# One load of the first batch's queries and keys for both attentions, pooled scores and value products in tiles of the array, and a new order

## The chip, the cores and the metric

The kernel runs on one core of a Trainium2 chip. The metric is the device time of one execution in microseconds; less is better. The core's engines are TensorE (PE), VectorE (DVE), ScalarE (ACT), GpSimd (POOL) and SyncE (SP), which issues most transfers here. Each engine runs its instructions in the order of the program and waits for the others through semaphores.

## The reference

Inputs `q`, `k`, `v` have shape (4, 8, 576, 64): batch, heads, sequence, head size.

```python
def _attn_ref(q, k, v):
    factor = 4
    # pooled: means over 4 tokens, full softmax attention over 144 positions, each result used for 4 tokens
    q_d, k_d, v_d = (x.reshape(B, H, Sd, factor, D).mean(axis=3) for x in (q, k, v))
    out_up = np.repeat(sm_attn(q_d, k_d, v_d), factor, axis=2)
    # local: each token attends to the 7 tokens with |distance| < 4
    mask = np.abs(pos[:, None] - pos[None, :]) < factor
    out_local = softmax(where(mask, scale * q @ k.T, -1e9)) @ v
    return out_up + out_local

x = attn_out.transpose(0, 2, 1, 3).reshape(2304, 512)
x = np.maximum(x @ w_in1, 0) ** 2 @ w_out1      # 512 -> 2048 -> 512
out = softplus(x @ w_in2) @ w_out2              # 512 -> 2048 -> 512
```

## The kernel before

One program does the attention and two MLP layers. The MLP's numbers are split into a high and a low half, so each product is three matmuls.

- **Token groups.** The 2304 tokens fall into five groups of `BLOCKS = [8, 6, 8, 8, 6]` blocks of 64. `STEPS` lists the MLP's work: a layer, a group and one of 16 slices of the hidden layer. `hidden` does a step's 12 hidden matmuls (tile `ph`), `activate` the activation and its high and low halves (`gh`, `gl`), and `outputs` the 12 output matmuls (`y`).
- **Weights.** `load_weights` loads half slices as raw 64-bit numbers (`raw`, three buffers, 512 KB each); `weight_job` converts one in seven instructions of ScalarE and VectorE (`f`, `r`, `w`) into a slot, and stores it to `wdram`, from where `weight_again` loads it for later uses.
- **Pooled attention** (`pooled`). 16 tasks, one for each batch and pair of heads. It sums queries and keys over four tokens (on VectorE, or for batch 1 on TensorE as `pqk`), makes two masked copies of the query sums (`qd`, with the constant `diag`, so that each holds one head's 64 rows and zeros), takes three score matmuls of 96 by 144 (`psc`), the softmax (`pn`, `pe`), six transposes (`ppp`), and two matmuls with the summed values (`vd`, `ppo`). Both heads' rows come out of one product, so a copy for each head picks its half into `up`.
- **Local attention** (`local`). 14 tasks, one for each block of groups 0 and 1. For four pairs of heads: scores in 64x64 tiles of the array (`lsc`), mask and softmax (`ls`, `ln`, `le`), transposes (`lpp`, `lpt`), four value products (`lav`), of which again each head's half is used, added to `up` on 64 partitions at a time (`lt`), and split into `xh` and `xl`, the MLP's input. Queries, keys and values of two blocks are one load each (`lq`, `lk`, `lv`). The tokens of groups 2 to 4 have local attention without matmuls (`direct`).
- **First buffers.** `lend` lets first loads use slots of weights and of inputs that are not needed yet.
- **The order.** Nothing is scheduled on the chip. While the program is built, the class `Order` follows a model of the engines and transfers: each stream says which engine it wants and for how long (`t_act`, `t_dve`, constants), `landed` models a transfer, and the piece that can start first is issued next. `either` lets it choose ScalarE or VectorE for a copy. The lists `POOLED` and `LOCAL` say from which step on a task may start. The model sets the order alone; the durations on the chip are what they are.

Of the kernel before, what the change touches and what calls it, by code (L numbers as in the profile page):

```python
# [28 lines left out]
KH = SP // 2  # L29
NF = DFF // 128  # L30
# [38 lines left out]
LOCAL = [(-18.9, -13), (-0.5, 5), (12, 58), (62, 86), (74, 92)]  # L69
# [16 lines left out]
WIN, HOT, COLD = 3.413, 3.1, 1.8  # L86

# [78 lines left out]
class Order:  # L166
# [66 lines left out]

def t_act(n):
    return 0.09 + n * 0.84e-3
# [12 lines left out]
def fused_kernel(ctx: ExitStack, tc: tile.TileContext, lq, lk, lv, dqk, dv, cdmask, pqk, pv, wts, cmask, cdiag, cident, out):  # L248
# [15 lines left out]
    diag = const.tile([128, 2], F32, name="diag")  # L264
# [12 lines left out]
    r_in = ring(att, "in", [128, 2 * S], BUFS["in"])  # L277
# [3 lines left out]
    r_qd = ring(att, "qd", [128, 2 * SP], 2)  # L281
# [17 lines left out]
    def copy(out, in_, scale=1.0):  # L299
        if order.chosen == "act":  # L300
            act.activation(out=out, in_=in_, func=AF.Copy, scale=scale)  # L301
        elif isinstance(scale, float):
            dve.tensor_copy(out=out, in_=in_)  # L303
        else:
            dve.tensor_scalar(out=out, in0=in_, scalar1=scale, scalar2=None, op0=ALU.mult)
# [139 lines left out]
    def lend():  # L445

        for p in range(LENT):
# [3 lines left out]
            x, y = both[:, :1024], both[:, 1024:]  # L451
            if p < NP:
                first_bufs["q", p] = Guest(x[:, :2 * NP * QB], lent[k])
                first_bufs["v", p] = Guest(y[:KH], lent[k])
            else:
                first_bufs["pv", 0] = Guest(x[:KH], lent[k])
        for p, r in enumerate((r_xh[1], r_xl[1])):
# [3 lines left out]
            first_bufs["in", 2 + p] = Guest(x[:, :2 * S], host)  # L461
            first_bufs["k", p] = Guest(x[:, 2 * S:2 * S + 2 * NP * KW], host)
# [6 lines left out]

    loads_direct = Event()  # L470
# [17 lines left out]
    def load_tasks():  # L488
        todo = [(mask, cmask)]
        for x, y in ((diag, cdiag), (ident, cident)):  # L490
            t = yield "sp", 0.06
            sp.dma_start(out=x, in_=y)
            order.landed(t, 65536)
        for (kind, at, hp, i, _), ev in zip(tasks, arrived, strict=True):
            if kind == "d":
                continue
            if kind == "l":
# [17 lines left out]
            else:  # L515
                two = at * NP + hp
                t = yield "sp", 0.06, *room(r_in, "in", two)
                ev.buf = take_for(r_in, "in", two)
                sp.dma_start(out=ev.buf.tile, in_=pqk[at * NP + hp])
                ev.at = order.landed(t, 128 * 4 * 2 * S)  # L520
# [24 lines left out]
    def pooled(b, hp, banks, ev, pace):  # L545

        on_pe = b in SUMS_ON_PE
# [540 lines left out]
```

## Time and profile before

| | |
|---|---|
| Median of 3 runs | 913.7 us (911.52 to 915.76) |
| Profiled execution | 916.07 us, of which the span of the instructions is 914.3 us |
| Busy: TensorE, VectorE, ScalarE, GpSimd | 882.6, 628.9, 507.8, 70.0 us |
| Granted TensorE clock, mean | 0.991 of full speed |
| Data moved by DMA | 179.51 MB |

A busy share is an average over stages. The rows further down are from this execution; times in them are us from the start of its span, and what a row calls PEld is the load of a matmul's fixed operand.

### The profile page before, as it was taken

To read this page: it belongs to the slowest core of one execution; us is meant where nothing else is said; L and a number is where in the kernel's file an instruction comes from. 1 tells how busy PE (TensorE), PEld (TensorE's weight loads), DVE (VectorE), ACT (ScalarE), POOL (GpSimd) and SP (SyncE) were. 2 spreads that over 40 slices of the span, in tenths; PEclk is the share of its full clock that TensorE was granted. 3 is DMA by queue.
4 is the path that set the end of the run, shared out by engine and by line. 5 is a ranking of instruction groups with operands and counts; after the bars stand their busy time and mean duration, and the time that the engine had idled before them with its cause. 6 is when DMAs were issued, how large, how long until landed. Compare 5 with 4: busy or idle time off the path is not lost.

```text
span 914.3 us, 12634 instructions
## 1 busy us (share of the span) xinstructions
PE 882.6 (97%) x4528; PEld 764.1 (84%) x4528; DVE 628.9 (69%) x1105; ACT 507.8 (56%) x1141; POOL 70.0 (8%) x136
## 2 busy tenths in 40 slices
PE   2989999999999999999999999999999999999997
PEld 2778879998888878888888888888999888988886
DVE  3798997899999999998777998986211224222222
ACT  3877876766887886554344544443333325544443
POOL 0000000000000000121111121101120010000000
PEclk9799999999999999999999999999999999999999
DMA  8958968884956873597776577740870262233001
GB/s 215 261 184 270 317 213 310 272 296 149 351 192 220 273 275 151 183 335 261 237 256 224 171 250 242 261 153 30 297 249 24 74 202 94 63 99 127 24 0 47
DMA packets 50091, 179.51 MB, mean 196 GB/s; under 512 B 5762, under 2 KB 6146, under 8 KB 50028
## 3 DMA queue, kind: packets, MB, share of 16 engines
q1 hardware_dynamic: 31020, 109.48, 35.6%
q0 software_dynamic: 19008, 69.21, 23.4%
q8 instruction: 36, 0.59, 0.3%
q14 instruction: 27, 0.22, 0.1%
HBM read 140.40 MB, written 38.27 MB: 195 GB/s over the span
## 4 chain that ended last, share of the span: by engine, by line
PE 83%; DVE 7%; DMA 6%; ACT 3%; issue 1%; SPq 0%; ACTq 0%
PE ph L861 39%; PE y L915 39%; DMA raw<-wts 3%; DMA first<-lk 1%; DMA w_first<-lq 1%; PE ppo L622 1%; DVE lt L701 1%; PE psc L580 1%; DVE f L375 1%; ACT le L669 1%; DVE vd L617 1%; ACT f L366 1%; PE ppp L608 1%; DVE xl L316 1%; PE dpp L803 1%
## 5 line engine op out<-in xcount | busy, mean ns | idle before, releaser
L861 PE MATMUL ph<-xh,w 128*128 128x512 f32 (+2 forms) x1304 | 397.4, 367 | 2.9 <-ACT xh L301 1.4
L861 PEld LDWEIGHTS ph<-xh,w 128*128 128x128 f32 x1304 | 240.9, 188 | 35.5 <-ACT xh L301 2.0
L861 PE MATMUL ph<-xl,w 128*128 128x512 f32 (+2 forms) x652 | 237.8, 365 | 1.0 <-DVE xl L316 1.0
L915 PE MATMUL y<-gh,w 128*128 128x512 f32 (+2 forms) x656 | 200.0, 367 | 0.0
L915 PE MATMUL y<-w,gh 128*128 128x512 f32 x576 | 179.5, 393 | 0.0
L316 DVE TENSOR_TENSOR gl<-g,gh 128x512 fp32r<-128x512 f32 (+2 forms) x163 | 101.9, 625 | 91.4 <-ACT gh L301 87.9
L861 PEld LDWEIGHTS ph<-xl,w 128*128 128x128 f32 x652 | 122.6, 188 | 16.9 <-DVE xl L316 1.4
L915 PEld LDWEIGHTS y<-gh,w 128*128 128x128 f32 x656 | 121.0, 188 | 14.4
L410 POOL DMA_DIRECT2D w<-wdram x132 | 69.8, 532 | 777.2 <-PE dpp L803 377.9
L915 PEld LDWEIGHTS y<-w,gh 128*128 128x128 f32 x576 | 106.7, 188 | 20.5
L915 PE MATMUL y<-gl,w 128*128 128x512 f32 (+2 forms) x328 | 119.1, 363 | 0.0
L915 PE MATMUL y<-w,gl 128*128 128x512 f32 x288 | 112.6, 391 | 0.0
L301 ACT ACTIVATE gh<-g 128x512 fp32r<-128x512 f32 (+2 forms) x127 | 72.8, 573 | 70.5 <-PE y L915 50.3
L884 DVE SCALAR_TENSOR_TENSOR g<-ph,g 128x512 f32<-128x512 f32 (+2 forms) x81 | 50.7, 626 | 89.1 <-ACT g L882 89.0
L878 ACT ACTIVATE g<-ph 128x512 f32<-128x512 f32 (+2 forms) x81 | 44.4, 549 | 117.0 <-PE ph L861 108.1
L873 ACT ACTIVATE g<-ph 128x512 f32<-128x512 f32 (+2 forms) x82 | 44.4, 542 | 112.5 <-PE ph L861 92.3
L915 PEld LDWEIGHTS y<-gl,w 128*128 128x128 f32 x328 | 61.7, 188 | 6.8
L915 PEld LDWEIGHTS y<-w,gl 128*128 128x128 f32 x288 | 54.1, 188 | 11.6
L366 ACT ACTIVATE f<-raw 128x512 f32<-128x512 f32 x64 | 42.6, 667 | 23.4 <-DMA raw<-wts 18.3
L303 DVE CAST gh<-g 128x512 fp32r<-128x512 f32 (+2 forms) x36 | 14.8, 410 | 51.2 <-PE y L915 43.5
L753 DVE TENSOR_TENSOR prod<-dqk 128x896 f32<-128x896 f32 x44 | 47.6, 1083 | 1.6 <-DMA dqk<-dqk 1.3
L876 ACT ACTIVATE g<-g 128x512 f32<-128x512 f32 (+2 forms) x82 | 47.4, 578 | 1.9
(99 smaller groups left out, 961.2 us busy)
## 6 DMA issues: line engine op xcount, KB each, us to landing
w<-wdram POOLq DMA_DIRECT2D x132, 512.0 KB, 4.3
raw<-wts SPq DMA_DIRECT2D x64, 512.0 KB
wdram<-w SPq DMA_DIRECT2D x64, 512.0 KB
dqk<-dqk SPq DMA_DIRECT2D x11, 896.0 KB
in<-pqk SPq DMA_DIRECT2D x14, 576.0 KB
dv<-dv SPq DMA_DIRECT2D x11, 640.0 KB
out<-o SPq DMA_DIRECT2D x18, 256.0 KB
pv<-pv SPq DMA_DIRECT2D x15, 288.0 KB
```

The lines of the kernel that those rows point to most:

```text
L301: act.activation(out=out, in_=in_, func=AF.Copy, scale=scale)
L303: dve.tensor_copy(out=out, in_=in_)
L316: dve.tensor_tensor(out=out, in0=whole, in1=high.bitcast(F32), op=ALU.subtract)
L366: act.activation(out=f.tile, in_=high.bitcast(F32), func=AF.Abs, scale=REBIAS)
L410: nc.gpsimd.dma_start(out=weights[slot][:, half], in_=wdram[c, half])
L753: dve.tensor_tensor(out=p4, in0=k4[:, :, tok:tok + TAPS, :], in1=q4[:, tok].unsqueeze(2).to_broadcast([128, 2, TAPS, D]), op=ALU.mult)
L861: pe.matmul(ph.tile[:, :n], w, y, start=(k == 0), stop=(k == len(prs) - 1))
L873: act.activation(out=o, in_=h, func=AF.Relu)
L876: act.activation(out=o, in_=o, func=AF.Square)
L878: act.activation(out=o, in_=h, func=AF.Abs)
L884: dve.scalar_tensor_tensor(out=o, in0=h, scalar=0.0, in1=o, op0=ALU.max, op1=ALU.add)
L915: pe.matmul(o, wt, y, start=(begin and k == 0), stop=(end and k == 2))
```

## The change

- The first batch's queries and keys were loaded twice: once for the pooled tasks (`pqk`) and once in blocks for the eight local blocks of group 0 (`lq`, `lk`). Now `pqk` carries three zero columns between queries and keys (`QKW = S + FCT - 1`), and the eight blocks read their queries and windows of keys from the four pooled tiles. These four loads come first in SP's queue, and each local block of group 0 waits for all four. The tiles lie in lent weight slots, with the sums and the softmax of the same task beside them.
- The pooled scores are six matmuls, each of one head's 64 rows and 64 query columns, instead of three on masked copies; `qd` and `diag` are gone. The three windows of 64 queries overlap and start 40 apart; 48 columns of each are used.
- The pooled and the local value products run per head, on 64 columns of the array, so both heads' results land on their own partitions: one copy into `up` and one addition into `lt` instead of two each.
- The planner's numbers change: slower transfers, 32 columns more for an MLP matmul, shorter pieces of TensorE, and the first entry of `LOCAL`.

```diff
-LOCAL = [(-18.9, -13), (-0.5, 5), (12, 58), (62, 86), (74, 92)]
+LOCAL = [(-17, -13), (-0.5, 5), (12, 58), (62, 86), (74, 92)]
...
-        self.dma = max(self.dma, self.issue + 0.65) + size / 3.6e5
-        return self.dma + 0.9
+        self.dma = max(self.dma, self.issue + 1.2) + size / (2.4e5 if self.dma < CROWDED else 3.3e5)
+        return self.dma + 1.3
...
+def t_pe(n):
+    return (n + 32) / 2.4e3
...
-                first_bufs["q", p] = Guest(x[:, :2 * NP * QB], lent[k])
-                first_bufs["v", p] = Guest(y[:KH], lent[k])
+                first_bufs["in", p] = Guest(both[:, :2 * QKW], lent[k])
+                first_bufs["in", p].left = 1 + BLOCKS[0]
+                s0 = 2 * QKW
+                first_bufs["qkd", p] = Guest(both[:, s0:s0 + 2 * SP], lent[k])
+                first_bufs["pe", p] = Guest(both[:, s0 + 2 * SP:s0 + 5 * SP], lent[k])
             else:
-                first_bufs["pv", 0] = Guest(x[:KH], lent[k])
+                for two in range(2):
+                    first_bufs["v", two] = Guest(both[:KH, two * 1024:two * 1024 + 1024], lent[k])
         for p, r in enumerate((r_xh[1], r_xl[1])):
             b = r.take("first")
             host = Host(b)
             x = b.tile.bitcast(F32).rearrange("p h n -> p (h n)")
-            first_bufs["in", 2 + p] = Guest(x[:, :2 * S], host)
-            first_bufs["k", p] = Guest(x[:, 2 * S:2 * S + 2 * NP * KW], host)
+            for two in range(2):
+                first_bufs["pv", 2 * p + two] = Guest(x[:KH, two * 1024:two * 1024 + 1024], host)
...
+        for p, ev in enumerate(first_pairs):
             t = yield "sp", 0.06
-            sp.dma_start(out=x, in_=y)
-            order.landed(t, 65536)
+            ev.buf = first_bufs["in", p]
+            sp.dma_start(out=ev.buf.tile, in_=pqk[p])
+            ev.at = order.landed(t, 128 * 8 * QKW)
...
+            if kind == "l" and not i:
+                if at % 2 == 0:
+                    t = yield "sp", 0.06, *room(r_v, "v", at // 2)
+                    bv = take_for(r_v, "v", at // 2)
+                    bv.left = 2
+                    sp.dma_start(out=bv.tile[:KW], in_=lv[at // 2])
+                    vthere = order.landed(t, KW * 4096)
+                ev.buf = None, None, bv, at % 2
+                ev.at = 0.0
+                ev.v.at = vthere
...
-            copy(qk3[:, 1], src[:, 1])
+            t = yield either, t_either(288)
+            copy(qk.tile, sums.tile[:, :2 * SP])
...
-        qd4 = qd.tile.rearrange("p (i a q) -> p i a q", i=3, a=2)
-        for a in range(2):
-            t = yield either, (0.31, 0.28)
-            copy(qd4[:, :, a, :], src[:, 0, :].rearrange("p (i q) -> p i q", i=3), scale=diag[:, a:a + 1])
-        if on_pe:
-            sums.free = t
-        t = yield "pe", 0.75, banks
+            t = yield "dve", t_dve(1152), ev, pace, *room(r_s, "qkd", two), *room(r_e, "pe", two), r_n
+            qk, e, n = take_for(r_s, "qkd", two), take_for(r_e, "pe", two), r_n.take("pn")
+            x4 = halves().rearrange("p a (g j) -> p a g j", j=FCT)
+            dve.tensor_reduce(out=qk.tile.rearrange("p (a g) -> p a g", a=2), in_=x4, axis=AX.X, op=ALU.add)
+            if b:
+                ev.buf.free = t
+            else:
+                used_once(t, ev.buf)
+
+        t = yield "pe", 0.5, banks
         sc = bank(banks, "psc")
-        sc3 = sc.tile[:96, :3 * SP].rearrange("p (i k) -> p i k", i=3)
+        sc3 = sc.tile[:, :3 * SP].rearrange("p (i k) -> p i k", i=3)
         for i in range(3):
-            pe.matmul(sc3[:, i, :], qd4[:, i].rearrange("p a q -> p (a q)"), qk3[:, 1, :], start=True, stop=True)
-        qk.free = qd.free = t
+            for p in (slice(0, 64), slice(64, 128)):
+                pe.matmul(sc3[p, i, :], qk.tile[p, i * RUN:i * RUN + 64], qk.tile[p, SP:], start=True, stop=True)
+        qk.free = t
...
-                pe.transpose(pp.tile[:KH, i * 96:(i + 1) * 96], e3[:96, i, a * KH:(a + 1) * KH], ident[:96, :96])
+                pe.transpose(pp.tile[:KH, i * 128:(i + 1) * 128], e3[:, i, a * KH:(a + 1) * KH], ident)
...
-            copy(pt3[:, a, :], pp.tile[:KH, :288])
+            used = pp.tile[:KH, :3 * (176 - RUN)].rearrange("p (i x) -> p i x", i=3)
+            used = used[:, :, :128].rearrange("p i (h q) -> p i h q", h=2)[:, :, :, :48]
+            copy(pt3[:, a, :].rearrange("p (i h q) -> p i h q", i=3, h=2), used)
...
-        t = yield "pe", 0.98, banks
+        t = yield "pe", 0.66, banks
         po = bank(banks, "ppo")
         for a in range(2):
-            pe.matmul(po.tile[:, :288], vd.tile[:, a, :], pt3[:, a, :], start=(a == 0), stop=(a == 1))
+            pt4 = pt3[:, a, :].rearrange("p (i h q) -> p h i q", i=3, h=2)
+            for h in range(2):
+                pe.matmul(po.tile[64 * h:64 * h + 64, :SP], vd.tile[:, a, 64 * h:64 * h + 64], pt4[:, h],
+                          start=(a == 0), stop=(a == 1))
         vd.free = pt.free = t
-        for j in range(2):
-            t = yield either, t_either(144)
-            p0 = 64 * j
-            copy(ups[b].tile[p0:p0 + 64, hp, :].rearrange("p (i q) -> p i q", i=3),
-                 po.tile[p0:p0 + 64, :288].rearrange("p (i a q) -> p i a q", i=3, a=2)[:, :, j, :])
+        t = yield either, t_either(144)
+        copy(ups[b].tile[:, hp, :], po.tile[:, :SP])
...
-        t = yield "pe", 0.86, ev, pace, banks, r_s, r_e, r_n, r_t
+        t = yield "pe", 0.62, ev, pace, banks, r_s, r_e, r_n, r_t, *([] if i else first_pairs)
         sc, s, e, n, o = bank(banks, "lsc"), r_s.take("ls"), r_e.take("le"), r_n.take("ln"), r_t.take("lt")
         bq, bk, bv, at = ev.buf
-        q = bq.tile.rearrange("p (w q) -> p w q", q=QB)
+        if i:
+            qs = [bq.tile[:, w * QB:w * QB + QB] for w in range(at * NP, at * NP + NP)]
+            ks = [bk.tile[:, w * KW:w * KW + KW] for w in range(at * NP, at * NP + NP)]
+        else:
+            qs = [x.buf.tile[:, blk * QB:blk * QB + QB] for x in first_pairs]
+            ks = [x.buf.tile[:, S + blk * QB:S + blk * QB + KW] for x in first_pairs]
         sc4 = sc.tile[:, :NP * KW].rearrange("p (h k) -> p h k", h=NP)
         for h in range(NP):
-            w = at * NP + h
             for p in (slice(0, 64), slice(64, 128)):
-                pe.matmul(sc4[p, h], q[p, w], bk.tile[p, w * KW:w * KW + KW], start=True, stop=True)
-        used_once(t, bq, bk)
+                pe.matmul(sc4[p, h], qs[h][p], ks[h][p], start=True, stop=True)
+        used_once(t, *((bq, bk) if i else (x.buf for x in first_pairs)))
...
-            pe.matmul(av.tile[:, h * 128:(h + 1) * 128], bv.tile[:KW, (at * NP + h) * 128:(at * NP + h + 1) * 128],
-                      pt.tile[:KW, h * 128:(h + 1) * 128], start=True, stop=True)
+            for a in range(2):
+                v0, q0 = (at * NP + h) * 128 + a * 64, h * 128 + a * QB
+                pe.matmul(av.tile[a * 64:a * 64 + 64, h * QB:(h + 1) * QB], bv.tile[:KW, v0:v0 + 64],
+                          pt.tile[:KW, q0:q0 + QB], start=True, stop=True)
...
-        for hh in range(2):
-            t = yield "dve", t_dve(256), up_ready[b]
-            p = slice(64 * hh, 64 * hh + 64)
-            dve.tensor_tensor(out=o4[p], in0=av5[p, :, hh], in1=u4[p].to_broadcast([64, NP, QB // FCT, FCT]),
-                              op=ALU.add)
+        t = yield "dve", t_dve(256), up_ready[b]
+        dve.tensor_tensor(out=o4, in0=av.tile[:, :NP * QB].rearrange("p (h g j) -> p h g j", h=NP, j=FCT),
+                          in1=u4.to_broadcast([128, NP, QB // FCT, FCT]), op=ALU.add)
...
-            t = yield "pe", 12 * n * 0.4219e-3, half_ready if s < SPLIT else x_ready[x], w_ready[fill_of[s], 0], r_h
+            t = yield "pe", 12 * t_pe(n), half_ready if s < SPLIT else x_ready[x], w_ready[fill_of[s], 0], r_h
```

On SP, at the start of the program (`w_first` and `first` are lent buffers), there stood

```order
L519 DMA in<-pqk 128x1152
L525 DMA w_first_88<-pv 72x1024
L529 DMA mask<-cmask 128x210
L519 DMA in<-pqk 128x1152
L525 DMA pv<-pv 72x1024
L504 DMA w_first_84<-lq 128x512
L507 DMA first<-lk 128x560
L510 DMA w_first_84<-lv 70x1024
L519 DMA first<-pqk 128x1152
L525 DMA pv<-pv 72x1024
L519 DMA first<-pqk 128x1152
L525 DMA pv<-pv 72x1024
```

and now stand

```order
L503 DMA w_first_83<-pqk 128x1158
L503 DMA w_first_84<-pqk 128x1158
L503 DMA w_first_85<-pqk 128x1158
L503 DMA w_first_86<-pqk 128x1158
L547 DMA first<-pv 72x1024
L551 DMA mask<-cmask 128x210
L547 DMA first<-pv 72x1024 x3
L513 DMA w_first_87<-lv 70x1024 x2
L513 DMA v<-lv 70x1024 x2
L541 DMA in<-pqk 128x1158
L547 DMA pv<-pv 72x1024
L541 DMA in<-pqk 128x1158
```

The four pairs have moved to the front, all loads of `lq` and `lk` for group 0 are gone, and behind the rows shown the raw weights follow at once; before, three more pairs of blocks and one `pqk` followed first.

On TensorE, just ahead of the first hidden matmul (`ph`), there stood

```order
L608 MATMUL ppp<-ident,pe 72x96 x3
L690 MATMUL lav<-lpt,w_first_85 128x128 x4
L622 MATMUL ppo<-ppt,vd 128x288 x2
L682 MATMUL lpp<-ident,le 70x128 x8
L690 MATMUL lav<-lpt,w_first_85 128x128 x4
L690 MATMUL lav<-lpt,w_first_86 128x128 x4
L654 MATMUL lsc<-k,w_first_86 64x70 x8
L654 MATMUL lsc<-k,w_first_87 64x70 x16
L861 MATMUL ph<-xh,w_79 128x256
```

and now stand

```order
L723 MATMUL lav<-lpt,v 64x64 x8
L584 MATMUL pqk<-in,ident 128x288 x4
L713 MATMUL lpp<-ident,le 70x128 x4
L584 MATMUL pqk<-in,ident 128x288 x4
L723 MATMUL lav<-lpt,v 64x64 x8
L713 MATMUL lpp<-ident,le 70x128 x8
L605 MATMUL psc<-qkd 64x144 x12
L723 MATMUL lav<-lpt,v 64x64 x16
L891 MATMUL ph<-xh,w_78 128x256
```

All eight value products of group 0 (`lav`) and two score groups of the second batch (`psc`) now come ahead of the first hidden matmul; before, five value products did.

On TensorE, around a value product (`ppo`) of the third batch between two steps of the MLP, there stood

```order
L915 MATMUL y_2475<-gh,w_1472 128x512
L915 MATMUL y_2475<-gl,w_1472 128x512
L915 MATMUL y_2475<-gh,w_1472 128x512
L622 MATMUL ppo<-ppt,vd 128x288 x2
L861 MATMUL ph<-xh,w_974 128x384
L861 MATMUL ph<-xl,w_974 128x384
```

and now stand

```order
L891 MATMUL ph<-xh,w_80 128x384 x2
L891 MATMUL ph<-xl,w_80 128x384
L891 MATMUL ph<-xh,w_80 128x384
L651 MATMUL ppo<-ppt,vd 64x144 x4
L891 MATMUL ph<-xh,w_947 128x384
L891 MATMUL ph<-xl,w_947 128x384
```

The product is four matmuls on 64 columns of the array instead of two on 128, and stands alone between full-array matmuls, as before.

## Rows read from the trace of the kernel before

**Rows 1.** The profile's page: span, and busy time of each engine

```profile
span 914.3 us, 12634 instructions
PE 882.6 (97%) x4528; PEld 764.1 (84%) x4528; DVE 628.9 (69%) x1105; ACT 507.8 (56%) x1141; POOL 70.0 (8%) x136
```

**Rows 2.** Busy time by stage: stage, its length, engines, TensorE clock, DMA share, GB/s

```profile
0.00:51.00 51.00, 31.04 (x252) 25.57 (x252) 30.59 (x76) 30.63 (x114) 0.20 (x4) 0.87 0.83 225
51.00:140.00 89.00, 82.56 (x554) 70.05 (x555) 81.96 (x198) 69.00 (x226) 0.00 (x0) 1.00 0.77 252
140.00:240.00 100.00, 100.00 (x530) 93.80 (x529) 91.69 (x160) 69.76 (x133) 0.00 (x0) 1.00 0.77 267
240.00:350.00 110.00, 109.57 (x526) 92.45 (x525) 104.54 (x193) 90.33 (x198) 0.00 (x0) 1.00 0.71 252
350.00:700.00 350.00, 350.00 (x1683) 301.61 (x1682) 259.66 (x377) 158.63 (x316) 55.06 (x104) 1.00 0.64 213
700.00:914.30 214.30, 209.43 (x991) 180.60 (x989) 60.45 (x105) 89.48 (x161) 14.78 (x28) 1.00 0.24 78
...
30.00:51.00 21.00, 17.71 (x166) 14.92 (x164) 18.95 (x53) 17.80 (x65) 0.00 (x0) 0.88 0.75 235
```

**Rows 3.** Chain of work, shares by line: 51 to 140, 140 to 240, 240 to 350, 350 to 600

```profile
by line: DMA raw<-wts 15.8%; PE ph L861 9.6%; ACT le L669 6.7%; DVE f L375 5.7%; DVE lt L701 4.9%; PE pqk L557 4.7%; DVE f L372 3.5%; ACT f L366 3.4%; PE y L915 3.3%; issue 3.0%; DVE xl L316 2.8%; ACT pe L591 2.7%; DVE vd L617 2.5%; DVE ls 
...
by line: PE ph L861 53.3%; PE y L915 46.9%
...
by line: PE y L915 26.8%; PE ph L861 26.4%; DMA raw<-wts 14.8%; DVE g L884 3.4%; DVE w L316 2.3%; PE psc L580 2.0%; DVE vd L617 1.9%; ACT f L366 1.8%; DVE prod L753 1.8%; PE ppo L622 1.8%; issue 1.7%; ACT g L882 1.6%; ACT g L880 1.5%; DVE x
...
by line: PE y L915 47.9%; PE ph L861 47.2%; PE dpp L803 1.6%; PE ppo L622 1.6%; PE psc L580 1.2%; PE ppp L608 0.8%
```

**Rows 4.** Chain of work in the opening: start, length, what

```profile
3.90 10.50 DMA w_first<-lq
14.42 13.07 DMA first<-lk
```

**Rows 5.** Groups by line and shape: count, busy us and mean ns, idle before

```profile
L701 DVE TENSOR_TENSOR lt<-lav,up 64x256 f32<-64x256 f32 x28 | 11.3, 419 | 0.5
...
L301 ACT ACTIVATE qd<-qkd,diag 128x144 f32<-128x144 f32 x24 | 9.0, 406 | 15.1 <-DVE qkd L568 15.1
L301 ACT ACTIVATE up<-ppo 64x144 f32<-64x144 f32 x26 | 7.3, 281 | 8.3 <-PE ppo L622 8.1
```

**Rows 6.** Timeline: first two reductions on VectorE, first hidden matmul on TensorE

```profile
7.55 1.35 DVE L568 TENSOR_REDUCE qkd<-in 128x288 f32<-128x1152 f32 x1 [7.55 <-DMA in<-pqk]
11.96 1.35 DVE L568 TENSOR_REDUCE qkd<-in 128x288 f32<-128x1152 f32 x1 [3.05 <-DMA in<-pqk]
...
51.08 0.38 PE L861 MATMUL ph<-xh,w 128*128 128x256 f32 x1 [0.96 <-ACT xh L301]
```

**Rows 7.** One chain piece, then TensorE's timeline around small groups: start, length

```profile
215.37 2.72 PE y L915 x12
...
111.67 0.71 PE L654 MATMUL lsc<-k,q 64*64 64x70 f32 x16
...
112.64 0.39 PE L915 MATMUL y<-gl,w 128*128 128x512 f32 x1
...
114.95 0.39 PE L915 MATMUL y<-gh,w 128*128 128x512 f32 x1
115.27 1.20 PE L654 MATMUL lsc<-k,q 64*64 64x70 f32 x32
...
116.73 0.40 PE L915 MATMUL y<-gl,w 128*128 128x512 f32 x1
...
241.79 0.90 PE L580 MATMUL psc<-qkd,qd 128*96 128x144 f32 x6
...
242.76 0.39 PE L915 MATMUL y<-gl,w 128*128 128x512 f32 x1
...
255.54 1.13 PE L622 MATMUL ppo<-ppt,vd 72*128 72x288 f32 x4
...
256.69 0.34 PE L861 MATMUL ph<-xl,w 128*128 128x384 f32 x1
```

More of the change, by code (lines that the diff above doesn't have):

```diff
@@ L29 @@
 KH = SP // 2
+RUN = (SP - 64) // 2
+QKW = S + FCT - 1
 NF = DFF // 128
@@ L86 @@
 WIN, HOT, COLD = 3.413, 3.1, 1.8
+CROWDED = 25.0
 def plan_weights():
@@ L297, in fused_kernel, with copy @@
     either = ("act", "dve")
-    def copy(out, in_, scale=1.0):
+    def copy(out, in_):
         if order.chosen == "act":
-            act.activation(out=out, in_=in_, func=AF.Copy, scale=scale)
-        elif isinstance(scale, float):
+            act.activation(out=out, in_=in_, func=AF.Copy)
+        else:
             dve.tensor_copy(out=out, in_=in_)
-        else:
-            dve.tensor_scalar(out=out, in0=in_, scalar1=scale, scalar2=None, op0=ALU.mult)
     def times(a, b):
@@ L468, in room @@
         return [] if (kind, at) in first_bufs else [r]
+    first_pairs = [ev for x, ev in zip(tasks, arrived) if x[:2] == ("p", 0)]
     loads_direct = Event()
@@ L489, in load_tasks @@
         todo = [(mask, cmask)]
-        for x, y in ((diag, cdiag), (ident, cident)):
+        t = yield "sp", 0.06
+        sp.dma_start(out=ident, in_=cident)
+        order.landed(t, 65536)
+        for p, ev in enumerate(first_pairs):
             t = yield "sp", 0.06
-            sp.dma_start(out=x, in_=y)
-            order.landed(t, 65536)
+            ev.buf = first_bufs["in", p]
+            sp.dma_start(out=ev.buf.tile, in_=pqk[p])
+            ev.at = order.landed(t, 128 * 8 * QKW)
         for (kind, at, hp, i, _), ev in zip(tasks, arrived, strict=True):
@@ L516, in load_tasks @@
                 two = at * NP + hp
[L517 to L520, printed above, removed]
+                if at:
+                    t = yield "sp", 0.06, r_in
+                    ev.buf = r_in.take("in")
+                    sp.dma_start(out=ev.buf.tile, in_=pqk[at * NP + hp])
+                    ev.at = order.landed(t, 128 * 8 * QKW)
                 late = i in DIRECT
@@ L547, in pooled, with halves @@
         on_pe = b in SUMS_ON_PE
+        two = b * NP + hp
+        def halves():
+            return ev.buf.tile.rearrange("p (a x) -> p a x", a=2)[:, :, :S]
         if hp == 0:
@@ L590, in pooled @@
         for i in range(3):
-            act.activation(out=e3[:96, i, :], in_=sc3[:, i, :], func=AF.Exp, scale=k,
+            act.activation(out=e3[:, i, :], in_=sc3[:, i, :], func=AF.Exp, scale=k,
                            bias=nm[:, i:i + 1], accum_out=sm[:, i:i + 1])
```

49 lines of the change are left out of this document (19 added, 30 removed).

## The prediction

> **What bounds the kernel now.** I read the busy times by stage first [rows 2], then the chain of work by stage [rows 3], then the opening inside it [rows 4, 6]. The page alone [rows 1] would mislead: TensorE shows 97% busy, but that mixes stretches with different limits.
>
> In 140 to 240 us TensorE is busy all the time [rows 2], and the chain holds nothing but hidden-layer and output matmuls (53.3% and 46.9%) [rows 3]. From 350 to 600 the chain is again TensorE's, 95% of it MLP and 5% small attention matmuls. There only TensorE's own work counts. In 240 to 350 the chain is mixed: 53% MLP matmuls, 14.8% loads of raw weights, VectorE pieces; VectorE is 104.5 of 110 us busy, so it limits nearly as much as TensorE does. Before 140 TensorE is not the limit: in 51 to 140 the MLP holds 12.9% of the chain, and VectorE is busy 82.0 of 89 us. In 0 to 51 there is no MLP work; the first hidden matmul starts at 51.08 [rows 6]. VectorE is busy 30.6 of these 51 us, so it idles 20.4. The chain names why: it runs through the load of one pair of blocks' queries (10.5 us) and through that of the next pair's keys (13.1 us), and both end only at 27.5 [rows 4]. In 30 to 51 VectorE is 18.95 of 21 us busy, ScalarE 17.8.
>
> So up to 140 the kernel runs at VectorE's pace, work plus idle time: 112.5 us of work and 27.4 of idle. Whatever shortens either brings forward the point where TensorE takes over.
>
> **The loads.** Ahead of the first weights SP had queued, by the shapes in the code, 7466 KB; now it is 6203 KB: four loads of queries and four of keys (2144 KB) are gone, one more of the second batch's pairs and one of its values (867 KB) have moved ahead, and small ones changed. At the stage's 225 GB/s [rows 2] the 1263 KB are 5.7 us. What matters more is order. Before, the second pair's reduction waited until 11.96, the first's until 7.55 [rows 6], because values and the mask stood between; the third and fourth pair came behind a pair of blocks' loads. Now all four pairs come first: three more of 579 KB at 225 GB/s, 2.6 us each, put the fourth at 7.55 + 7.9 = 15.4 us. From then on VectorE and ScalarE have four pooled tasks and eight local blocks to work on.
>
> **VectorE until the first hidden matmul.** In the order before, VectorE's instructions up to 51 us add up to 35.0 us by the mean durations of their kinds, and the trace shows 30.6 busy [rows 2], since neighbours overlap: factor 0.874. In the new order 93 rows stand ahead of what the first hidden matmul can't pass (the copy of the eighth block's transposed weights is the last of them): 41.9 us listed, 36.6 busy. So more attention is done before the MLP starts: on TensorE all eight blocks' value products stand ahead of it, before it was five. Of the 36.6, the first nine rows (5.9 listed, 5.2 busy) are done by 15.4 us. The other 31.4 run at the density of 30 to 51, 90% [rows 2]: 34.9 us, first hidden matmul at 50.3. That is hardly earlier than 51.1, but VectorE has idled 13.7 us then, not 20.4: **-6.7 us**. Bounds: without any stall it starts at 46.8 (idle 10.2, so -10.2); with twice the stalls at 54.7 (idle 18.1, -2.3).
>
> **Work removed.** Each local block's two additions on 64 partitions (419 ns each, 28 in all) [rows 5] become one on 128; its columns are the same 256, so I keep 419 ns: 0.42 us less for each of 14 blocks, all on VectorE before 140. Each pooled task loses two masked copies of the queries (406 ns, nearly all on ScalarE) and one of two copies of its output (281 ns on ScalarE) [rows 5]. Where the sums come from TensorE (second batch), one copy grows from 144 to 288 columns, about 0.1 us. The planner gives VectorE some of ScalarE's copies in exchange: in the new order the tenth low half of an activation stands at 117.5 us of listed VectorE work, before at 121.7. 4.2 x 0.874 = **-3.7 us**. From the thirtieth on the two orders are level (the fiftieth is 1.6 us later in the new one), so this is a gain of the first stage alone. VectorE's idle time in 51 to 140, 7.0 us, I leave as it is. ScalarE's saving counts for nothing, since ScalarE is busy 69 of 89 us there.
>
> **TensorE in its own stretch.** The pooled tasks of batches 3 and 4 lie behind 240, eight of them. A float32 matmul shows as two passes; a task's three score matmuls are six in the rows, and from the first of them to the second MLP matmul behind them it is 242.76 - 241.79 = 0.97, less 0.227 for one MLP matmul (2.72 / 12): 0.74, or 6 x 0.123, with nothing on top [rows 7]. The local scores, in 64x64 tiles, do have something on top: eight pairs (each matmul in two passes, so 16 rows) take 112.64 - 111.67 - 0.227 = 0.74, sixteen pairs 116.73 - 115.27 - 0.227 = 1.23, so a pair costs 0.061 and each group 0.25 more; and the group starts at 115.27, 0.09 after 114.95 + 0.227. **0.34 us a group** [rows 7]. The Trainium skill, TensorEngine Tiling (Array Packing), Key Properties, states that a change of the tiling mode drains the engine. By that rule, the trace agrees, with 0.34 us.
>
> Scores: a pair of 70 columns takes 0.061, and 0.123 x 70/144 = 0.060 is what one of the two would take alone, so the two run side by side. Pairs of 144 columns then take 0.74 a task as before, plus 0.34. Transposes: 128 columns for 96, 2 x 3 x 32 columns at 0.85 ns (0.123/144) = 0.16 more. Values: 256.69 - 255.54 - 0.174 (one 384-column matmul) = 0.97 before [rows 7]; halves of 144 columns side by side 0.49, plus 0.34: 0.14 less. A task costs 0.34 + 0.16 - 0.14 = 0.36 more, eight of them **+2.8 us**. Bounds: with no cost for the switch -2.6; with the value halves one after the other (no row shows two tiles that share their rows) another 0.49 a task, +6.7.
>
> **How much of the lead lasts.** The lead at 140 is 6.7 + 3.7 = 10.4. To keep it to step 50 VectorE must be as much ahead there: it has 5.3 (6.7 of idle less 1.6 x 0.874 of work put earlier), and 8.3 + 5.5 = 13.8 us of idle in 140 to 350 [rows 2] to squeeze. If half of the missing 5.1 is found, **+2.5** is given back. Bounds 0 and 5.1. Part of the switches in 240 to 350 then hides behind VectorE: 0.5 off.
>
> **Sum.** -6.7 - 3.7 + 2.8 + 2.5 - 0.5 = -5.6. The profiled execution took 916.07 us, a span of 914.3 [rows 1] and 1.8 around it; the median of the runs shown is 913.7, 0.26% lower. 914.3 - 5.6 = 908.7 of span, 910.5 for such an execution, **908.1** against the median.
>
> **Rivals.** (1) The lead lasts whole and the switches hide: -10.4 to -14, 900 to 903. For it: VectorE is busy only 260 of 350 us behind 350 [rows 2]; against it: 240 to 350 is tight. (2) The lead fades: VectorE and the raw weights hold 240 to 350, +5.1 holds, the value halves don't run side by side and nothing hides: -10.4 + 5.1 + 6.7 = +1.4, 911 to 915. That is also about what is left if the loading was hidden anyway, since the new order puts more work ahead of the first hidden matmul. (3) Slower: ScalarE's first weight conversion waits. Ahead of it ScalarE has 20 us of attention work that can start near 12, so it gets there near 33; the 6074 KB behind the first pair, at 225 GB/s, have landed at 35. Behind it, in order, stand the blocks' copies and high halves, VectorE's additions behind those, and TensorE's products behind both. Two us late is within the stalls that I count; each us beyond that is idle on both engines. The gain is gone 5.6 us later, and 0.5% is lost 10.2 us later, at a pace of some 165 GB/s: 920. Against it: the mean of 225 already includes the empty start. (4) A task's two head halves write one bank of the accumulator and run one after the other: 0.73 more a task, +5.9, so 914.0. The local scores write one bank in the same way, and 0.061 a pair speaks against it. The Trainium skill, TensorEngine Tiling (Array Packing), Gotcha 1: PSUM Pressure, states that row tiles can't use one bank at the same time. By that rule it would be 914.0; the trace here differs.
>
> **How the numbers follow.** 0.5% is about what a measurement of this kernel tells from no change: 909.1 and 918.3. The forecast gets 0.5 (own range 903 to 912), rival 1 0.2, rival 2 0.17, rival 3 0.08, rival 4 0.05. Faster: 0.35 of the forecast's 0.5 and rival 1, 0.55. Same: its other 0.15 and rivals 2 and 4, less 0.02 for their upper ends, 0.35. Slower: 0.1. The range leaves out the end of rival 1 and rival 3: 899 to 914.5.
>
> **What would show it.** Right: VectorE idles 11 to 16 us before the first hidden matmul, which starts within 47 to 54; the four reductions are done by 18; score and value groups show some 0.34 us beside their passes; TensorE is full from about 130 us on. Wrong: a wait of ScalarE for raw weights of over 3 us near 33; the start after 55; gaps on TensorE in 140 to 350 that weren't there; values at 0.98 us a task beside the switch.

## The result and the profile after

The changed kernel takes 902.38 us in the median of 4 runs (900.84 to 903.91), the kernel before 913.88 beside it: a ratio of 0.987, 95% interval 0.9845 to 0.9896. The forecast was 908.1. The sign was right and the size less than half of what was measured: the span fell by 12.2 us (914.3 to 902.1), not by 5.6.

The page of the profile after, its span and busy times, beside [rows 1]:

```profile
span 902.1 us, 13041 instructions
PE 884.2 (98%) x4800; PEld 755.0 (84%) x4800; DVE 630.1 (70%) x1105; ACT 483.6 (54%) x1071; POOL 70.0 (8%) x136
```

VectorE's total did not fall (628.9 before), since the planner gave it ScalarE's copies (ScalarE 507.8 to 483.6). The gain is a matter of when. Busy time by stage after, beside [rows 2], with the columns named there:

```profile
0.00:51.00 51.00, 40.69 (x408) 31.02 (x410) 37.11 (x97) 34.42 (x136) 0.20 (x4) 0.80 0.66 193
51.00:140.00 89.00, 86.86 (x685) 73.83 (x682) 82.24 (x186) 68.90 (x194) 0.00 (x0) 1.00 0.89 303
140.00:240.00 100.00, 100.00 (x524) 91.48 (x523) 98.68 (x179) 70.07 (x137) 0.00 (x0) 1.00 0.78 272
240.00:350.00 110.00, 110.00 (x548) 90.40 (x547) 106.60 (x183) 83.04 (x175) 0.00 (x0) 1.00 0.66 226
```

VectorE is busy 37.1 of the first 51 us (30.6 before), while TensorE's granted clock there fell from 0.87 to 0.80. Now the busy time of the MLP's matmuls alone, from the start to 140 and to 350 us, first the hidden (`ph`), then the output ones (`y`). Before:

```profile
0.00:140.00 140.00, 27.95 (x134) 21.62 (x135) 0.95 0.80 242
0.00:350.00 350.00, 137.90 (x648) 114.16 (x648) 0.98 0.76 252
...
0.00:140.00 140.00, 25.03 (x120) 19.20 (x120) 0.95 0.80 242
0.00:350.00 350.00, 130.24 (x594) 105.12 (x595) 0.98 0.76 252
```

After:

```profile
0.00:140.00 140.00, 36.84 (x185) 30.60 (x186) 0.93 0.80 263
0.00:350.00 350.00, 145.13 (x682) 120.61 (x683) 0.97 0.75 254
...
0.00:140.00 140.00, 31.50 (x156) 25.33 (x156) 0.93 0.80 263
0.00:350.00 350.00, 137.35 (x624) 110.51 (x624) 0.97 0.75 254
```

By 140 us 68.3 us of MLP work are done instead of 53.0: a lead of 15.4 us (forecast 10.4). By 350 us the lead is 14.3, at the end 12.2. The chain of work shows where TensorE has taken over: 36 hidden matmuls in a row from 122.72 us on, before 35 from 137.63. From 51 us up to that point TensorE is busy 69.6 of 71.7 us and VectorE 68.3, so after the change the point is a mark for the account and no sharp border. Up to these points VectorE's work and idle time, before and after:

```profile
137.63 6.36 PE ph L861 x35
0.00:137.63 137.63, 111.23 (x793) 93.25 (x793) 110.97 (x271) 99.16 (x337) 0.20 (x4) 0.95 0.80 244
```

```profile
122.72 6.26 PE ph L891 x36
0.00:122.72 122.72, 110.27 (x985) 87.57 (x986) 105.39 (x257) 91.02 (x305) 0.20 (x4) 0.92 0.79 252
```

VectorE's work fell by 5.6 us (110.97 to 105.39) and its idle time by 9.3 (26.7 to 17.3). 6.5 of the latter lie ahead of 51 us (20.4 to 13.9), 2.8 behind it (6.2 to 3.4). The two together are 14.9, about the lead, and the MLP work ahead of the two points is the same (50.6 and 50.1 us). In 51 to 140 the chain ran through raw weights for 15.8% [rows 3]; after, they are not among its lines down to 1.2%, and TensorE is:

```profile
by line: PE ph L891 33.7%; PE y L945 29.4%; PE pqk L584 4.6%; PE lav L723 4.1%; PE ppp L633 3.2%; PE ppo L651 2.9%; PE lsc L685 2.7%; PE lpp L713 2.3%; PE psc L605 2.0%; DVE xl L319 1.8%; ACT le L700 1.5%; DVE w L319 1.3%; DVE lt L731 1.2%;
```

Timeline after: the four reductions and the first hidden matmul, beside [rows 6], then the group of additions, beside [rows 5]:

```profile
5.31 2.78 DVE L594 TENSOR_REDUCE w_first<-w_first 128x288 f32<-128x1152 f32 x2 [5.31 <-DMA w_first<-pqk]
11.40 1.34 DVE L594 TENSOR_REDUCE w_first<-w_first 128x288 f32<-128x1152 f32 x1
...
51.84 0.38 PE L891 MATMUL ph<-xh,w 128*128 128x256 f32 x1
...
L731 DVE TENSOR_TENSOR lt<-lav,up 128x256 f32<-128x256 f32 x14 | 5.8, 422 | 3.3 <-PE lav L723 3.1
```

The fourth reduction starts at 11.40 us (forecast 15.4), and yet the first hidden matmul at 51.84, later than before. What lies between is the surprise of this case. Windows of the opening after; the columns are those of [rows 2], the clock is the last but two:

```profile
20.00:25.00 5.00, 2.84 (x26) 1.68 (x21) 4.61 (x14) 4.81 (x25) 0.00 (x0) 0.98 1.04 282
25.00:30.00 5.00, 5.00 (x46) 3.48 (x46) 3.36 (x10) 3.88 (x20) 0.00 (x0) 0.50 0.77 282
30.00:35.00 5.00, 5.00 (x58) 3.77 (x58) 3.14 (x11) 2.40 (x7) 0.00 (x0) 0.50 0.11 43
35.00:40.00 5.00, 5.00 (x70) 4.17 (x68) 2.94 (x9) 3.28 (x11) 0.00 (x0) 0.50 0.00 0
40.00:45.00 5.00, 5.00 (x25) 3.59 (x24) 4.51 (x15) 3.80 (x22) 0.00 (x0) 0.50 0.27 83
```

TensorE is busy without a gap at half its clock (1.2 of 2.4 GHz) from 25 to 45 us, and VectorE waits for it: of these 20 us it idles 6.05, and 5.8 of them end with a score, a value product or a transpose of the local blocks. Just before, TensorE had been busy 2.84 of 5 us. Its timeline there, and what the half clock costs one group (`pqk`, 4.21 us; at the full clock 2.11 in the filled kernel below):

```profile
20.23 1.96 PE L633 MATMUL ppp<-ident,w_first 128*72 128x128 f32 x12
24.34 0.84 PE L651 MATMUL ppo<-ppt,vd 72*64 72x144 f32 x8 [2.15 <-DVE ln L706]
...
40.85 4.21 PE L584 MATMUL pqk<-in,ident 128*128 128x288 f32 x8
```

Last, the switch of the array's mode that the forecast charged, on TensorE at two pooled groups, beside [rows 7]:

```profile
224.45 0.39 PE L945 MATMUL y<-gh,w 128*128 128x512 f32 x1
224.77 0.95 PE L605 MATMUL psc<-qkd 64*64 64x144 f32 x12
...
225.99 0.39 PE L945 MATMUL y<-gl,w 128*128 128x512 f32 x1
...
242.90 0.34 PE L891 MATMUL ph<-xh,w 128*128 128x384 f32 x1
243.17 0.71 PE L651 MATMUL ppo<-ppt,vd 72*64 72x144 f32 x8
...
244.09 0.34 PE L891 MATMUL ph<-xl,w 128*128 128x384 f32 x1
```

Scores: 225.99 - 224.77 - 0.227 = 0.99, and a start 0.09 late, 1.08 (forecast 0.74 + 0.34). Values: 244.09 - 243.17 - 0.174 = 0.75, and 0.10 late, 0.85 (forecast 0.49 + 0.34).

### The profile page after: what moved, and what is told of

Its sections match the earlier page's. It is cut to its first block, busy times and chain, and to the rows that moved or that the text cites. A ratio compares the mean times of both kernels' runs of the same rounds, so it can differ in the third digit from the quotient of the medians.

```text
span 902.1 us, 13041 instructions
## 1 busy us (share of the span) xinstructions
PE 884.2 (98%) x4800; PEld 755.0 (84%) x4800; DVE 630.1 (70%) x1105; ACT 483.6 (54%) x1071; POOL 70.0 (8%) x136
## 4 chain that ended last, share of the span: by engine, by line
PE 89%; DVE 6%; DMA 2%; ACT 2%; issue 1%; SPq 0%; ACTq 0%; DVEq 0%
PE y L945 40%; PE ph L891 40%; PE psc L605 2%; DMA raw<-wts 1%; PE pqk L584 1%; PE lav L723 1%; PE ppo L651 1%; PE ppp L633 1%; PE lpp L713 1%; PE lsc L685 1%; DVE do L826 1%; DVE gl L319 1%; DVE prod L819 1%; DVE dsc L790 1%; DVE prod L783 1%
## 5 line engine op out<-in xcount | busy, mean ns | idle before, releaser
L945 PEld LDWEIGHTS y<-gh,w 128*128 128x128 f32 x656 | 121.0, 188 | 15.8 <-issue 1.4
L306 ACT ACTIVATE gh<-g 128x384 fp32r<-128x384 f32 (+2 forms) x116 | 66.0, 569 | 91.9 <-PE y L945 57.2
L308 DVE CAST gh<-g 128x512 fp32r<-128x512 f32 (+2 forms) x47 | 19.4, 412 | 64.6 <-PE y L945 56.6
L906 ACT ACTIVATE g<-g 128x512 f32<-128x512 f32 (+2 forms) x82 | 47.4, 579 | 1.7
L910 ACT ACTIVATE g<-g 128x512 f32<-128x512 f32 (+2 forms) x81 | 47.3, 583 | 2.0
```

The lines of the kernel that those rows point to most:

```text
L306: act.activation(out=out, in_=in_, func=AF.Copy)
L906: act.activation(out=o, in_=o, func=AF.Square)
L910: act.activation(out=o, in_=o, func=AF.Exp, scale=-1.0)
L945: pe.matmul(o, wt, y, start=(begin and k == 0), stop=(end and k == 2))
```

## The experiments

All times are medians. The kernel before was measured again beside each of four sets of runs, at 915.4 to 917.0 us, and 913.9 beside the changed kernel. So a difference between sets is given as a range, by the ratios and by the medians; within a set it is one number.

### Which part gives it: numbers, load or tiles

**Numbers.** The changed kernel with the planner's former numbers, and the kernel before with the new ones:

```diff
-        self.dma = max(self.dma, self.issue + 1.2) + size / (2.4e5 if self.dma < CROWDED else 3.3e5)
-        return self.dma + 1.3
+        self.dma = max(self.dma, self.issue + 0.65) + size / 3.6e5
+        return self.dma + 0.9
...
-    return (n + 32) / 2.4e3
+    return n * 0.4219e-3
...
-LOCAL = [(-17, -13), (-0.5, 5), (12, 58), (62, 86), (74, 92)]
+LOCAL = [(-18.9, -13), (-0.5, 5), (12, 58), (62, 86), (74, 92)]
```

> The changed kernel with the planner's former numbers for transfers, MLP matmuls and the first local tasks. Theory A (loads and tiles give the time, the numbers hardly any): 903 to 905 us, TensorE full from about 125 us. Theory B (the 3.6 us less idle of VectorE in 51 to 140 and more come from the numbers): 907 to 910 us, with ScalarE waiting 3 us or more for raw weights before 140.

Measured: 911.58 us, ratio 0.9937 (0.991 to 0.9964).

> The kernel before with only the planner's new numbers. Theory A: 911 to 914 us. Theory B: 906 to 909 us, VectorE's idle time in 51 to 140 down from 7.0 to about 3.5 us.

Measured: 919.91 us, 1.0033 (1.0013 to 1.0053). Neither theory holds: the new numbers lose a little alone and are worth 6 to 9 us with the new parts. In this run VectorE is busy 37.0 of the first 51 us: the new order alone takes away 6.4 us of the idle time whose end the forecast had put down to the loads. It gains nothing by it: in 51 to 140 VectorE then idles 10.3 us (7.0 before), and the clock there is 0.94, with 0.50 in 60 to 65.

```profile
0.00:51.00 51.00, 35.32 (x286) 28.48 (x286) 37.00 (x98) 33.34 (x132) 0.20 (x4) 1.00 0.86 243
51.00:140.00 89.00, 83.42 (x532) 70.44 (x531) 78.71 (x180) 68.48 (x200) 0.00 (x0) 0.94 0.75 255
```

**The load.** Array tiles and new numbers, with queries and keys loaded twice:

```diff
-                pe.matmul(sc4[p, h], qs[h][p], ks[h][p], start=True, stop=True)
+                pe.matmul(sc4[p, h], q[p, w], bk.tile[p, w * KW:w * KW + KW], start=True, stop=True)
```

> Array tiles and the new numbers, but queries and keys of the first batch loaded twice as before. If the single load gives the 6.3 us less idle of VectorE ahead of the first hidden matmul: 908 to 911 us, VectorE idle some 19 to 21 us of the first 51. If the order alone gives it: 902 to 904 us.

Measured: 901.39 us, 0.9825 (0.9793 to 0.9857), 1 to 4 us below the changed kernel. As it stands, the single load gives nothing, as the second theory of that run says. The clock stays at 1.00 in this run:

```profile
0.00:51.00 51.00, 35.47 (x413) 26.20 (x414) 37.22 (x96) 33.29 (x133) 0.20 (x4) 1.00 0.88 245
```

**The tiles.** The changed kernel with masked scores, whole value products and two copies or additions:

```diff
-            for a in range(2):
-                v0, q0 = (at * NP + h) * 128 + a * 64, h * 128 + a * QB
-                pe.matmul(av.tile[a * 64:a * 64 + 64, h * QB:(h + 1) * QB], bv.tile[:KW, v0:v0 + 64],
-                          pt.tile[:KW, q0:q0 + QB], start=True, stop=True)
+            pe.matmul(av.tile[:, h * 128:(h + 1) * 128], bv.tile[:KW, (at * NP + h) * 128:(at * NP + h + 1) * 128],
+                      pt.tile[:KW, h * 128:(h + 1) * 128], start=True, stop=True)
...
+        for a in range(2):
+            t = yield either, (0.31, 0.28)
+            copy(qd4[:, :, a, :], src[:, 0, :].rearrange("p (i q) -> p i q", i=3), scale=diag[:, a:a + 1])
```

> The single load and the new numbers, but masked scores, whole value products and two copies or additions each as before. 5.8 us of additions on VectorE come back before 140, and 2.9 us of switches on TensorE behind 240 go: 904.5 to 907 us if VectorE's work sets the pace before 140; 899 to 901 us if it doesn't.

Measured: 913.53 us, 0.9972 (0.9947 to 0.9997), 9 to 11 us above the changed kernel, more than either theory said. Both theories left the clock out: in this run it is 0.97 in the first 51 us (0.80 in the changed kernel). The parts do not add up: the numbers (6 to 9 us) and the tiles (9 to 11) are each needed for most of the gain of 11.5. Then one half of that edit each:

> The changed kernel with the local value products of the two heads of a pair whole again (128 by 128, both heads' cross terms), and so the local addition again in two halves: 14 more VectorE instructions of about 0.42 us (5.9 us), 4 per block in the local attention. The pooled tiles and the single load stay. Leaving the heads together in both attentions cost about 10 us. Theory B1 (VectorE's work on the way to full TensorE sets the pace, so instructions saved there count one for one): 906 to 909 us. Theory B2 (what counted are the masked copies in the chain of each pooled task, not the additions): 902 to 904.5 us.

Measured: 907.65 us, 0.9917 (0.9894 to 0.994): 4.3 to 5.3 us for 5.9 of VectorE's work, the time that B1 gave. That the additions alone cost it is not shown: the same edit makes the value products longer (two blocks take 1.95 us instead of 1.34 at clock 1.00), and the first hidden matmul starts at 56.52 instead of 51.84, in a stretch where VectorE also waits for TensorE.

> The changed kernel with only the pooled attention as before: masked copies of the pooled queries for each head, scores in 96 rows, value products whole and two copies out of them; the local value products stay apart. Theory B1 (VectorE's work counts one for one; the pooled copies are mostly ScalarE's): 903 to 906 us. Theory B2 (the masked copies between the sums and the scores lengthen each pooled task's chain, which holds the blocks behind it): 907 to 911 us.

Measured: 908.86 us, 0.993 (0.9908 to 0.9952), 5.5 to 6.5 us, as B2 gave it. Its mechanism is neither shown nor refuted. The MLP work by 350 us is 144.37 + 138.20 = 282.6 us, as much as the changed kernel's 282.5, but this run's clock in the first 51 us is 0.97, not 0.80. Beside the kernel of the next section, which keeps its clock at 1.00 and was measured in the same set, it takes 11.8 us more and has done 6.4 us less MLP work by 350 us (282.6 and 288.9). In 480 to 500 us TensorE is 17.58 us busy instead of 20.00, with this wait:

```profile
PE y L953 <- DVE xl L323: 2.4, 1, 2.4
```

So 2.4 us are one wait of the order that follows from the edit; the rest is not placed.

**One number.** The former landing estimate and the former place of the first blocks, with the new length of a matmul:

> The changed kernel with only the planner's former estimate of when a transfer has landed and the former place of the first blocks; the new estimate of a matmul's length stays. All three former numbers together gave 911.6 us, 9 us more than the changed kernel. Theory N1 (what the numbers give is a better order of the opening, so the landing estimate is what counts): 909 to 912 us, with the granted clock disturbed in the opening as there. Theory N2 (the matmul's length gives it, through the order in the middle, where 220 to 520 us lost some 4 us more): 902 to 905 us.

Measured: 910.58 us, 0.9951 (0.9932 to 0.997). N1: these two numbers cost 7 to 8 us, all three 6 to 9. So nearly all of what the numbers give comes from the two that set the order of the opening.

### The clock

The changed kernel, its 2.15 us gap filled:

```diff
         po = bank(banks, "ppo")
+        if b == 0 and hp == 2:
+            for _ in range(8):
+                pe.matmul(po.tile[:, :128], ident, ident, start=True, stop=True)
```

> The changed kernel, and nothing else but eight products of the identity with itself (128 columns each) ahead of the third pair's pooled value products in the first batch, where TensorE waited 2.15 us (22.2 to 24.3 us) and after which its granted clock stood at 0.50 until about 45 us. They go into the bank that those products then overwrite, and the planner does not count them, so the order of the instructions stays. They add about 1.7 us of TensorE work inside the wait. Theory C (the half clock from 25 to 45 us eats what the single load had given): the granted clock stays at or near 1.00 from 25 to 45 us, the transposes and products of the local blocks take about half as long there, VectorE's idle time in 25 to 45 us (about 6 us now) shrinks by 3 to 5 us, the first hidden matmul comes at 47 to 49 us, and the time is 897 to 900 us. Theory D (the opening is held by VectorE, ScalarE and the transfers, and the clock costs nothing): the clock rises but the first hidden matmul stays at 51 to 52 us and the time at 901 to 904 us. If the clock does not rise, the run says nothing on the two.

Measured: 897.04 us, 0.9806 (0.9784 to 0.9827), the fastest kernel of the study. Run again beside its control:

> The changed kernel with the gap filled, as before (897.0 us), beside the three others on the same chip, so that they are compared without a change of chip: 896 to 899 us by both theories.

Measured: 897.65 us, 0.9784 (0.9759 to 0.9809). Its windows and its timeline on TensorE:

```profile
20.00:25.00 5.00, 4.72 (x40) 3.57 (x38) 4.36 (x14) 4.92 (x24) 0.00 (x0) 1.00 1.02 280
25.00:30.00 5.00, 4.92 (x79) 3.68 (x76) 4.67 (x16) 4.82 (x23) 0.00 (x0) 1.00 0.82 309
30.00:35.00 5.00, 5.00 (x106) 4.16 (x104) 5.00 (x17) 4.85 (x14) 0.00 (x0) 1.00 0.08 30
35.00:40.00 5.00, 3.39 (x17) 2.45 (x16) 5.00 (x17) 5.00 (x26) 0.00 (x0) 1.00 0.33 105
40.00:45.00 5.00, 5.00 (x84) 4.07 (x82) 4.89 (x12) 4.40 (x12) 0.00 (x0) 1.00 0.93 259
...
22.49 1.95 PE L650 MATMUL ppo<-ident 128*128 128x128 f32 x16
24.72 0.47 PE L654 MATMUL ppo<-ppt,vd 72*64 72x144 f32 x4 [0.27 <-DVE vd L644]
...
38.69 2.11 PE L584 MATMUL pqk<-in,ident 128*128 128x288 f32 x8
...
45.04 0.39 PE L894 MATMUL ph<-xh,w 128*128 128x256 f32 x1
```

The filling takes 1.95 us of the wait, the clock stays at 1.00, VectorE idles 0.44 us in 25 to 45 instead of 6.05, and the first hidden matmul starts at 45.04. Theory C holds; the idle time fell by more than its 3 to 5 us, and the matmul came earlier than its 47 to 49. Beside the changed kernel, measured in another set, the filling is worth 5 to 8 us. The Trainium skill, TensorE: Matmul & The Clock Gate, HAM oscillation — how this bites in real kernels, says that waits between groups of matmuls can bring TensorE's clock down, so that the next group starts at the low rate; this trace agrees in kind, with 0.50 from 25 us on, behind one wait of 2.15 us, here for VectorE and shorter than the waits for DMA of some 3 to 5 us in the page's example.

The control is the same filling in the kernel with two loads:

> The kernel with the array tiles and the new numbers but with queries and keys still loaded twice, which kept its clock at 1.00 and gave 901.4 us, and now the same eight products of the identity ahead of the third pair's pooled value products as in the filled changed kernel. Control for that kernel. Theory C (the filling helps by the clock alone, and the single load is worth about 5 us once the clock holds): nothing to gain here, 900 to 904 us, so 4 to 6 us above the filled kernel with one load. If the filling helps in another way, by the order or the banks: 895 to 898 us.

Measured: 902.85 us, 0.9841 (0.9817 to 0.9865). The filling has no other use, and with the clock held the single load is worth 902.85 - 897.65 = 5.2 us.

### Do the former numbers cost by the clock?

The former order had its clock at 0.50 in 30 to 40 us too. I filled it at twenty places, then only where TensorE waited; the third run prices the first filling in the changed kernel.

```diff
         po = bank(banks, "ppo")
+        if b == 0:
+            for _ in range(3):
+                pe.matmul(po.tile[:, :128], ident, ident, start=True, stop=True)
...
         pp, pt = bank(banks, "lpp"), r_pt.take("lpt")
+        if g < 8:
+            for _ in range(3):
+                pe.matmul(pp.tile[:, :128], ident, ident, start=True, stop=True)
...
         av = bank(banks, "lav")
+        if g < 8:
+            for _ in range(3):
+                pe.matmul(av.tile[:, :128], ident, ident, start=True, stop=True)
```

> The changed kernel with all three of the planner's former numbers (which alone gave 911.6 us, its granted clock at 0.83, 0.50 and 0.65 in parts of the first 60 us), and with filling: three products of the identity with itself (about 0.21 us each at the full clock) ahead of the four pooled value products of the first batch and ahead of the transposes and the value products of the first eight local blocks, in the same banks, not counted by the planner, so that the order stays that of the former numbers. Theory N3 (the former numbers cost because their order leaves TensorE sparse and the clock falls): the clock is at or near 1.00 over the first 60 us and the time is 897 to 903 us. Theory N4 (their order itself is worse, by what waits on what): the clock holds and the time stays at 906 to 912 us.

Measured: 910.56 us, 0.9937 (0.9918 to 0.9956), clock 1.00.

> The changed kernel with the fuller filling (three products of the identity at each of twenty places, some 13 us), instead of the eight in its one gap. It prices the filling. Theory N4 needs the filling to be cheap: 896 to 900 us, as with the eight alone. Theory N3 needs it dear: 904 to 910 us.

Measured: 909.64 us, 0.9931 (0.9909 to 0.9953). The filling is dear: 11 to 13 us above the eight products in the gap, at a full clock. One of its windows:

```profile
30.00:35.00 5.00, 5.00 (x65) 4.62 (x64) 2.94 (x10) 0.90 (x3) 0.00 (x0) 1.00 0.34 130
```

TensorE is busy all the time and VectorE waits, as at half clock. So the run before it says nothing on its theories.

> The changed kernel with the planner's former numbers, filled only where TensorE waited in that order (1 to 7 products of the identity ahead of three pooled value products, four local value products and two local transposes, some 7 us in all instead of 13). Theory N3 (the former numbers cost because the clock falls, and the fuller filling paid for itself): the clock is at or near 1.00 in the first 60 us and the time is 897 to 904 us. Theory N4 (their order is worse at full clock too): 906 to 912 us with the clock held.

Measured: 909.75 us, 0.9924 (0.9899 to 0.9948), with a clock of 1.00 up to 60 us. VectorE is busy 41.8 of the first 51 us (39.7 without the filling), but in 45 to 85 us engines now wait for each other inside pooled tasks; two rows of its waits, which without the filling were 2.8 and 1.5 us:

```profile
ACT pe L616 <- DVE pn L612: 5.9, 3, 2.4
...
DVE pn L609 <- PE psc L605: 3.1, 3, 1.4
```

That speaks for N4: the former order is worse by what waits for what. Some 7 us of filling are in it, not all of it certain to be hidden, so part of what the numbers give may still be the clock's.

The kernel before, filled at its own places:

> The kernel before, with filling alone: fourteen products of the identity with itself ahead of the second pair's first pooled transposes (where TensorE waited 4.04 us and after which its granted clock was 0.50 from about 22 to 35 us), and three each at the places of the run above. If the former opening was held by TensorE's half clock too, the time falls by 3 to 6 us, to 908 to 911 us; if it was held by the loads and the masked copies, the clock rises and the time stays within 3 us of the kernel before, 911 to 917 us.

Measured: 917.59 us, 1.0009 (0.9995 to 1.0023), TensorE busy all of 20 to 45 us at clock 1.00; after the price found above this tells nothing.

> The kernel before, filled only where TensorE waited: fourteen products of the identity ahead of the second pair's first pooled transposes, and two each ahead of the transposes of three local blocks and the value products of four (some 6 us instead of 13). With the clock at or near 1.00: 908 to 911 us if the half clock held the former opening, 913 to 917 us if the loads and the masked copies held it.

Measured: 914.93 us, 1.0005 (0.9968 to 1.0042), from 912.44 to 922.87, and in the profiled run the clock fell to 0.50 at another place, 40 to 45 us. Whether the half clock held the kernel before stays open.

## Why the prediction was wrong

With the new numbers, four kernels give the parts: whole heads and two loads 919.9, whole heads and one load 913.5, tiles and two loads 901.4 (one set), tiles and one load 902.4 (its own set; 897.0 to 897.7 with the clock held). So the tiles are worth 18.5 us with two loads and 9 to 11 with one. The load is worth 6.4 us with whole heads, nothing with the tiles, and 5.2 with tiles and the clock held. The four do not run at one clock: in this order it is 1.00, 0.97, 1.00 and 0.80 in the first 51 us, and 0.94 in 51 to 140 for the first. Beside the filled kernel the tiles are worth 15 to 17 us with one load, so most of the difference between 18.5 and 9 to 11 goes with the clock. The prediction had it the other way: "The loads" were the largest term, and the tiles came to -3.7 + 2.8.

- **-6.7, idle time ahead of the first hidden matmul.** 20.4 to 13.9 us, so the size was right, and 36.6 us of work ahead of it was near 37.8. The cause was wrong, so that the size came out is luck: with two loads and the tiles VectorE idles 13.8, and with the new numbers alone 14.0. The loads did come early, but TensorE at half clock took their gain; with the clock held, VectorE idles 8.0 us ahead of the first hidden matmul. The clock of 0.87 in the opening stands in [rows 2], and the prediction makes no term of it. Of the two loads in [rows 4] only the second ends at 27.5; the first ends at 14.4.
- **"VectorE's idle time in 51 to 140, 7.0 us, I leave as it is." This step failed,** and it is the largest part of what the forecast missed: up to the takeover the idle time behind 51 us fell by 2.8. (Over the whole of 51 to 140 it is 6.8, as forecast, but half of that now lies behind the takeover, where it costs nothing.) VectorE's waits for ScalarE up to the takeover were 4.5 us in sum before and are 1.1 after; the longest of them before, then after:

```profile
DVE up L303 <- ACT up L301: 1.8, 1, 1.8
DVE pn L595 <- ACT pe L591: 1.5, 1, 1.5
...
DVE gh L308 <- ACT g L906: 0.6, 1, 0.6
```

So ScalarE's saved copies, which I counted at nothing, may be the cause; no run tried them alone, and it stays open.

- **-3.7, work removed: too small where it counts.** Up to its own mark, the tenth low half of an activation, it was -4.1, near the forecast. Up to the takeover, which comes later, it was -5.6. The additions alone are 28 of 419 ns against 14 of 422, 5.8 us. VectorE's work up to the mark, before and after, is the third of the busy times:

```profile
0.00:131.88 131.88, 106.55 (x771) 89.73 (x772) 105.40 (x259) 96.95 (x332) 0.20 (x4) 0.95 0.81 246
...
0.00:118.60 118.60, 106.15 (x955) 84.36 (x956) 101.27 (x248) 88.62 (x302) 0.20 (x4) 0.91 0.79 252
```

- **+2.8, the switches.** Scores and values take 1.08 and 0.85 us a task, as worked out from [rows 7] (1.08 and 0.83).
- **+2.5 and -0.5, the lead given back: too large.** 15.36 - 14.34 = 1.0 by 350 us and 2.1 behind it. With the switches 3.2 were lost, not 4.8.

Measured in all: -5.6 - 6.5 - 2.8 + 2.7 to the end = -12.2 (the lead by VectorE's account is 14.9). Of the 6.6 us that the forecast missed, 2.8 are the idle time left as it was, 2.1 the lead given back and 1.9 the work, less 0.2 for the first term. Rival 1's time came true, not its account: more lead, and not all kept. Rival 2 is refuted: TensorE is busy all of 240 to 350, and 14.3 us of lead are left at 350. Rival 3 is refuted: in the first 51 us no wait for raw weights is among ScalarE's, and in 51 to 140 it waits 1.4 us for them, before 3.6. Rival 4 is refuted: the scores' two halves, row tiles that write one bank, each on its own 64 partitions, take 0.74 us a task beside the switch, 6 x 0.123, what one half alone would. The Trainium skill, TensorEngine Tiling (Array Packing), Gotcha 1: PSUM Pressure, says that row tiles can't use one bank at the same time; the trace differs, with this number.

## What to carry to other kernels

Where an engine off the critical path has a gap just before a dense stretch, look at the clock granted behind it: an edit that shortens loads can open that gap and lose what it won. Filling that one wait gave 5 to 8 us; filling at twenty places took 11 to 13 us longer than that. Where an engine's pace holds a stage, count its removed instructions and its idle time up to the point where another engine takes over, not to a fixed step. Before two versions are compared, look at the clock of both: here it hid 5 to 8 us of what load and tiles gave.

## What the runs showed of the hardware that I had not expected

TensorE's granted clock went to 0.50 behind a wait of 2.15 us in a stretch where it had been busy 2.84 of 5 us, and stayed there while it was busy without a gap for 20 us, in small groups of attention matmuls. The same groups at clock 1.00 took half as long (`pqk` 4.21 and 2.11 us). Not every sparse stretch did this: with two loads TensorE was busy 2.94 of the 5 us from 45 us on, and the clock stayed at 1.00. Score and value products of two heads write one bank, each on its own 64 partitions, and run side by side, at the speed of one: 0.74 and some 0.5 us a task beside the switch of 0.34.
